# Attention and mixture of experts on one core: blocks gathered in quarters of rows and turned on VectorE, the norm's weight moved into the first layer's weights

## The chip, the cores and the metric

The kernel runs on one core of one Trainium2 chip. The metric is the time of one execution on the device in microseconds (us), the median over several runs; less is better.

The engines are named as in the profile: PE is TensorE's matmul (PEld its weight load), DVE is VectorE, ACT is ScalarE, POOL is GpSimd, SP is SyncE, which here only issues transfers. L711 is line 711 of the kernel before.

## The reference

Two stages. The first is linear attention without softmax over 8 batches, 8 heads, 576 positions and 64 dimensions, then a root-mean-square norm over the 64 dimensions with a weight `g_norm`:

```
kv  = einsum('bhsd,bhse->bhde', k, v)
out = einsum('bhsd,bhde->bhse', q, kv)
rms = sqrt(mean(out * out, axis=-1, keepdims=True) + 1e-6)
x   = out / rms * g_norm          # heads side by side: 4608 tokens x 512
```

The second is a mixture of experts: a token goes to one of 8 experts (a local gate may let it keep its predecessor's expert), and its output is

```
h      = maximum(x[b, s] @ w1[e], 0)      # 512 -> 1024
out    = p[e] * (h @ w2[e])               # 1024 -> 512
```

All data is float32. The kernel splits every operand of the expert layers in a high and a low part of type fp32r and adds three products (high·high, low·high, high·low).

## The kernel before

**Attention (about 0 to 130 us).** Groups of two batches: `kv` on PE (L346), turns of q (L406), the output (L427), and its sums of squares. The row of a token, not yet divided by its root mean square and without `g_norm`, is kept in `raw`, together with the reciprocals `r` of its 8 heads' root mean squares and 8 gates. 36 stores of 128 rows put them into the DRAM tile `xs`, 566 floats a row: 4 pieces of 128 values (two heads each) at a pitch of `PW` = 146, the reciprocals and gates in the space behind the first piece.

**Transfers on SP.** `fetch` (L169) issues everything that is not indexed on SP, in program order, and makes each wait for the seventh one before it (`LANES` = 7). Beside that the completion of transfers from SP and ACT is counted on eight semaphores in turn, and a transfer waits until the one before it on its semaphore has landed.

**Experts.** Expert 0 is done first, in four blocks, while routing ends. The other seven follow by load, as ranks 1 to 7 with the fixed widths 768, 704, 640, 608, 608, 576 and 512 tokens, that is 6, 6, 5, 5, 5, 5 and 4 blocks of up to 128 tokens. A rank takes its blocks in two parts, `la` and `lb` (3+3, 3+3, 2+3, 2+3, 2+3, 2+3 and 2+2): `first_wide` multiplies all tokens of `la` with w1, `second` multiplies each block with w2 (24 matmuls of 512 columns, 8 values of f by 3 products), then the same for `lb`. `ma` and `mb_` are the parts of the next rank.

A block passes these steps:

- `gather`: one indirect DMA on POOL (L711) brings 128 rows of 566 floats into a tile `xr` (6 buffers).
- `scale`: DVE multiplies the 512 values by the reciprocals (L724) and picks the gate `pe` (L1185, L1187).
- `turn`: four PE transposes of 128x128 into the PSUM tile `pt` (L734); ACT writes the high part, `pt` times `gcol` (L738, `gcol` is `g_norm` per partition); DVE writes the low part (L739). The results are `xh`, `xl` for one part of a rank and `yh`, `yl` for the other.
- at the end of `second`, ACT multiplies by the gate into `ot` (2 buffers, L909), and POOL scatters its rows to the output (L910).

The turns of the next part stand as hooks between the matmuls of `second`, so PE does a turn between two f.

**Weights.** Each rank needs 8 tiles of 128x1024 (4 of w1, 4 of w2). `wload` brings one into a staging tile `wst` (4 buffers), `wsplit` writes the high part on ACT (L221) and the low part on DVE (L225); the next load is issued when a staging tile comes free. A tile of w1 holds 128 consecutive input dimensions, one a partition.

**The order.** From expert 0's last block on the program stands in `manual_schedule`: PE, ACT, DVE and POOL execute in the order in which the code is written. The hooks and the places of the gathers in the loop over r set it. Before that, in the routing, the table `PASS` says at which point which helper runs.

Of the kernel before, what the change touches and what calls it, by code (L numbers as in the profile page):

```python
# [22 lines left out]
def kernel(  # L23
# [13 lines left out]
    P = 128  # L37
# [28 lines left out]
    XW = NP * PW - 2 * NG  # L66
# [7 lines left out]
    xs = dram.tile([NT, XW], F32, name="xs")  # L74
# [25 lines left out]
    gidr = const.tile([P, NR * KBM], I32, name="gidr")  # L100
    sidr = const.tile([P, NR * KBM], I32, name="sidr")
# [88 lines left out]
    def wfetch(t, e, i):  # L190

        if not isinstance(e, int):
            e = bass.ds(e, 1)
            if i < NW1:
# [6 lines left out]
        if i < NW1:  # L201
            fetch(t, w1[e, i * P:(i + 1) * P, :])
        else:
            f0 = (i - NW1) * 2 * P
            fetch(t.rearrange("p (a d) -> p a d", a=2),
                  w2[e, f0:f0 + 2 * P, :].rearrange("(a p) d -> p a d", p=P))

# [3 lines left out]
    def wsplit(e, i, two=False):  # L211
# [9 lines left out]
        nc.scalar.copy(hi, t)  # L221
        wt[e, i] = (hi, lo)

        def low(engine=nc.vector):
            engine.tensor_sub(lo, t, hi.bitcast(F32))  # L225
# [247 lines left out]
    def rows_out(g, raw, ms, kk):  # L473
# [49 lines left out]
        nc.vector.tensor_copy(raw[:, 0:n, XO + P:XO + P + H], r)  # L523
        nc.vector.tensor_mul(raw[:, 0:n, XO + P + H:XO + P + H + E], pe,
# [4 lines left out]
    def store(n=C):  # L529

        for _ in range(n):
            if not to_store:
# [4 lines left out]
                  raw[:, c, XO:XO + XW])  # L537
# [54 lines left out]
    def by_rank(ids, gi, si):  # L592
# [8 lines left out]
        make_idx(gi, si, tr, sm)  # L601

    def route(g, kk):
# [60 lines left out]
        def perms(n0, n1):  # L664
# [3 lines left out]
            if last:  # L668
# [7 lines left out]
                else:  # L676
                    assert "ranks" in done
                    by_rank(tid[:, ns], gidr, sidr)
# [9 lines left out]
        if last:  # L688
            ids(*cuts[1])
            yield  # L690
            perms(*cuts[1])
        elif g == 0:
# [16 lines left out]
    def gather(xr, idx, rows=NT, pin=False):  # L709
        assert len(stored) * P >= rows  # L710
        i = nc.gpsimd.indirect_dma_start(  # L711
            out=xr[:, 0:XW], out_offset=None, in_=xs[0:rows],
# [5 lines left out]

    def scale(xr, engine=None):

        xv = xr.rearrange("p (a w) -> p a w", a=NP)[:, :, 0:P].rearrange(
            "p a (x d) -> p a x d", x=2)
        r = xr[:, P:P + H].rearrange("p (a x) -> p a x", x=2)
# [3 lines left out]
    def gate(xr, e):  # L727
        return xr[:, P + H + e:P + H + e + 1]

    def turn(xr, xh, xl, t0, psum, tag="pt", pin=False, late=False):  # L730

        pt = psum.tile([P, ND, P], F32, name="pt", tag=tag)
        for d in range(ND):
            i = nc.tensor.transpose(pt[:, d], xr[:, d * PW:d * PW + P], ident)  # L734
# [156 lines left out]
    def products(pool, w, hh, hl, t0, pe, idx, psum, hooks=(), pin=False, m=P, late=False):  # L891
# [15 lines left out]
        def finish():  # L907
            ot = pool.tile([P, DM], F32, name="ot", bufs=2)
            nc.scalar.activation(ot[0:m], po[0:m], AF.Copy, scale=pe[0:m])  # L909
            nc.gpsimd.indirect_dma_start(  # L910
# [5 lines left out]
    def second(*a, **kw):  # L916
        products(*a, **kw)()
# [19 lines left out]
    def block(pool, w, t, pe, idx, psh, pst, psy, hooks, hs=None):  # L937
# [31 lines left out]
        second(pool, w, hh, hl, 0, pe, idx, psy, fs)  # L969
# [49 lines left out]
    PASS = dict(at.split(":") for at in "a0:2s22 a4:3 a6:223o33 b2:o b3:t c1:3 c2:x c3:3 c5:33T d1:3 d3:3 d4:f3 d5:r d8:3 d11:y d13:l d14:F".split())  # L1019

    def at(k):

        def do():
            for what in PASS[k]:
# [64 lines left out]
    def stream_block(op, e, t, idx):  # L1089
# [3 lines left out]
        def piece(i):  # L1093
# [3 lines left out]
            nc.scalar.copy(hi, st)  # L1097
            nc.vector.tensor_sub(lo, st, hi.bitcast(F32))
# [74 lines left out]
    class Block:  # L1173


        def __init__(self, r, kb, m=P):
            self.r, self.c, self.m = r, (r - 1) * KBM + kb, m

        def gather(self):
            self.xr = gather(xtile(xp, XB), cidx(gidr, self.c))  # L1180

        def scale(self):
            scale(self.xr)
            t = xp.tile([P, NR], F32, name="gs", bufs=2)
            nc.vector.tensor_mul(t, self.xr[:, P + H + 1:P + H + E], oneh[:, self.r - 1])  # L1185
# [3 lines left out]
        def turn(self, xh, xl, t0):  # L1189
            turn(self.xr, xh, xl, t0, ps_t)  # L1190
# [4 lines left out]
    def parts(r):  # L1195
# [3 lines left out]
        bl = [Block(r, k, min(P, n - k * P)) for k in range(-(-n // P))]  # L1199
# [12 lines left out]
    block(z, w, fourth, gate(fourth[0], 0), cidx(sidx, 3), ps_h, ps_t, ps_y,  # L1212
# [98 lines left out]
```

## Time and profile before

| measure | before |
|---|---|
| median of 3 runs | 599.58 us (597.09 to 602.48) |
| the profiled execution | 600.44 us, of which the span of its profile 598.7 us |
| PE busy | 558.3 us (93%) |
| DVE busy | 273.7 us (46%) |
| ACT busy | 237.9 us (40%) |
| POOL busy | 133.3 us (22%) |
| moved by DMA | 94.26 MB, mean 157 GB/s |

Busy times count instructions that are executing; issuing of transfers is in none of the five, but POOL's indirect DMAs, whose descriptors POOL writes itself, are in POOL's. A row of a timeline gives the start, the duration, the engine, the line, the operation with its tiles and, in brackets, how long the engine was idle before it and what ended that. On PE the durations of matmuls that follow one another overlap, so what one costs there is the distance between starts.

### The profile page before, as it was taken

The numbers are of one execution on the slowest core, as the hardware profiler recorded it, in microseconds if no ns is written. First come the engines' busy times: TensorE is split into PE (matmuls) and PEld (weight loads), VectorE is DVE, ScalarE is ACT, GpSimd is POOL, SyncE is SP. The second block draws the span as 40 slices with busy tenths as digits, with TensorE's granted clock in tenths as the row PEclk, the third lists the DMA queues.
The fourth block names the chain that finished last, engine by engine and source line by source line (L and its number), as shares of the span: only waits on it lengthen the run. The fifth ranks groups of instructions, "written<-read, shape, count | busy, mean of one in ns | idle before, by whom it ended". The sixth has DMA issues, their size and how long they took to land. (4 is left out here: it accounts for less than half of the span.)

```text
span 598.7 us, 12747 instructions
## 1 busy us (share of the span) xinstructions
PE 558.3 (93%) x5285; PEld 496.0 (83%) x5285; DVE 273.7 (46%) x539; ACT 237.9 (40%) x433; POOL 133.3 (22%) x200
## 2 busy tenths in 40 slices
PE   3888877869999999999999999999999999999996
PEld 3777766759887989898988898989798989988895
DVE  1128477769876436244342534444443625352410
ACT  1677766552254234233432333333333433442220
POOL 3333343233343021120302020202122011201001
PEclk9988889879999999999999999999999999999999
DMA  8999999570676334330623263515352444331000
GB/s 275 326 322 342 303 374 373 198 249 21 223 270 253 108 126 126 106 121 18 197 96 109 71 181 89 146 52 177 109 154 76 124 141 119 113 104 42 18 19 29
DMA packets 39906, 94.26 MB, mean 157 GB/s; under 512 B 5791, under 2 KB 5791, under 8 KB 39840
## 3 DMA queue, kind: packets, MB, share of 16 engines
q1 hardware_dynamic: 32320, 72.31, 36.3%
q0 software_dynamic: 6304, 21.04, 11.2%
q8 instruction: 43, 0.70, 0.5%
q10 hardware_dynamic: 1216, 0.02, 0.1%
q14 instruction: 23, 0.19, 0.1%
HBM read 73.48 MB, written 20.53 MB: 157 GB/s over the span
## 5 line engine op out<-in xcount | busy, mean ns | idle before, releaser
L921 DVE SCALAR_TENSOR_TENSOR hl<-ph,hh 128x384 fp32r<-128x384 f32 (+3 forms) x92 | 53.3, 580 | 144.1 <-ACT hh L920 118.1
L910 POOL DMA_INDIRECT out_dram<-ot,sidr x36 | 35.4, 984 | 336.5 <-ACT ot L909 336.5
L920 ACT ACTIVATE hh<-ph 128x384 fp32r<-128x384 f32 (+3 forms) x92 | 46.9, 510 | 130.2 <-PE ph L882 126.3
L909 ACT ACTIVATE ot<-py,pe 128x512 f32<-128x512 f32 (+2 forms) x39 | 26.8, 687 | 112.2 <-issue 54.9
L711 POOL DMA_INDIRECT xr<-xs,gidr x36 | 38.7, 1075 | 11.5 <-issue 9.9
L346 PE MATMUL po<-vt,kt 64*64 64x64 f32 x1152 | 25.9, 239 | 14.8 <-DMA vt<-in_v_dram 9.2
L471 DVE TENSOR_REDUCE ms<-sq 128x9 f32<-128x576 f32 x32 | 23.1, 750 | 32.4 <-POOL sq L466 26.6
L346 PEld LDWEIGHTS po<-vt,kt 64*64 64x64 f32 x1152 | 23.5, 153 | 14.1 <-issue 13.0
L427 PE MATMUL po<-kvb,qT 64*64 64x73 f32 x1024 | 28.2, 241 | 6.4 <-issue 5.6
L466 POOL TENSOR_TENSOR sq<-raw 128x576 f32<-128x576 f32 x16 | 20.5, 1285 | 60.5 <-ACT raw L436 21.0
L427 PEld LDWEIGHTS po<-kvb,qT 64*64 64x64 f32 x1024 | 22.7, 143 | 13.5 <-issue 9.2
L739 DVE SCALAR_TENSOR_TENSOR yl<-pt,gcol,yh 128x512 fp32r<-128x512 f32 x20 | 15.0, 751 | 36.7 <-ACT yh L738 36.7
L433 ACT COPY raw<-po 128x876 f32<-128x876 f32 (+1 forms) x32 | 20.8, 649 | 17.9 <-PE po L427 17.3
L367 POOL COPY kvb<-kvp 64x128 f32<-64x128 f32 x64 | 22.0, 343 | 17.4 <-ACT kvp L350 9.6
L724 DVE TENSOR_TENSOR xr<-xr 128x512 f32<-128x512 f32 x37 | 25.3, 683 | 0.6 <-DMA xr<-xs,gidr 0.6
L734 PEld LDWEIGHTS pt<-ident,xr 128*128 128x128 f32 x152 | 18.6, 140 | 6.6 <-issue 1.7
L734 PE MATMUL pt<-ident,xr 128*128 128x128 f32 x152 | 22.9, 273 | 1.0 <-issue 0.9
L406 PE MATMUL pq<-ident,qt 128*128 128x128 f32 x128 | 21.7, 318 | 2.0 <-ACT ql L387 1.0
L876 PE MATMUL py<-w_0h,hh 128*128 128x512 f32 (+2 forms) x58 | 23.5, 404 | 0.0
L876 PE MATMUL py<-w_1h,hh 128*128 128x512 f32 (+2 forms) x58 | 23.2, 399 | 0.0
L738 ACT ACTIVATE yh<-pt,gcol 128x512 fp32r<-128x512 f32 x20 | 13.8, 689 | 23.4 <-PE pt L734 23.4
L882 PE MATMUL py<-w_0h,hl 128*128 128x512 f32 (+2 forms) x58 | 22.9, 394 | 0.0
(359 smaller groups left out, 1661.4 us busy)
## 6 DMA issues: line engine op xcount, KB each, us to landing
wst<-in_moe_w_dram SPq DMA_DIRECT2D x64, 512.0 KB, 3.6
xs<-raw SPq DMA_DIRECT2D x36, 283.0 KB, 3.7
kt<-in_k_dram SPq DMA_DIRECT2D x32, 288.0 KB, 4.7
vt<-in_v_dram SPq DMA_DIRECT2D x32, 288.0 KB, 5.2
qt<-in_q_dram SPq DMA_DIRECT2D x32, 288.0 KB, 5.4
xr<-xs,gidr POOLq DMA_INDIRECT x36
out_dram<-ot,sidr POOLq DMA_INDIRECT x36
out_dram<-ot,si POOLq DMA_INDIRECT x3
```

Source lines behind the costliest of these rows:

```text
L346: nc.tensor.matmul(pk[half(x ^ b), x, 0:D], ks[b][half(x), cd], vs[b][half(x), cd], start=(c == 0), stop=(c == C - 1))
L427: nc.tensor.matmul(po[half(b), r, o:o + HW], lhsT[half(r), half(x)], kvb[half(r), slot(x, b):slot(x, b) + HW], start=True, stop=True)
L471: nc.vector.tensor_reduce(mss[g][:, :, 2 * n + x], sqs.pop((s, x)), axis=AX.X, op=ALU.add)
L711: i = nc.gpsimd.indirect_dma_start(out=xr[:, 0:XW], out_offset=None, in_=xs[0:rows], in_offset=bass.IndirectOffsetOnAxis(ap=idx, axis=0), ...
L724: (engine or nc.vector).tensor_mul(xv, xv, r.unsqueeze(3).to_broadcast([P, NP, 2, D]))
L734: i = nc.tensor.transpose(pt[:, d], xr[:, d * PW:d * PW + P], ident)
L876: mm = nc.tensor.matmul(ps, ah, bh, start=(first and i == 0), stop=False)
L882: nc.tensor.matmul(ps, al, bh, start=False, stop=(last and i == n - 1))
L909: nc.scalar.activation(ot[0:m], po[0:m], AF.Copy, scale=pe[0:m])
L910: nc.gpsimd.indirect_dma_start(out=outf, out_offset=bass.IndirectOffsetOnAxis(ap=idx[0:m], axis=0), in_=ot[0:m], in_offset=None, bounds_ch ...
L920: nc.scalar.activation(hh, ps, AF.Relu)
L921: nc.vector.scalar_tensor_tensor(hl, ps, 0.0, hh.bitcast(F32), op0=ALU.max, op1=ALU.subtract)
```

## The change

- **Rows of xs** get all 584 floats (4 x 146) in place of 566. The reciprocals of heads 2n and 2n+1 stand behind piece n, so a quarter of a row has its values and its two reciprocals; the 8 gates (`XE`) stand at a place of their own.
- **Gather by quarters.** A block of ranks 2 to 7 (30 blocks) is no longer brought by one indirect DMA of 128 rows x 566, but by `gather4`: four of 128 x 146, the u-th with the index table `gid4[:, u]`, and one of 128 x 8 for the gates. `gid4` is arranged so that partition 32q+k holds quarter q of the tokens 32u+k. Rank 1 (6 blocks) and expert 0 are gathered whole.
- **Turn on VectorE.** `turn4` takes the place of the four PE transposes in these 30 blocks: one DVE STREAM_TRANSPOSE in squares of 32x32 from `xr` into `xT` (one buffer), an ACT copy into the high part, a DVE subtraction into the low part. All are in SBUF. Input dimensions then lie on partitions in another order, (quarter, k mod 32) in place of 128 consecutive ones.
- **w1 in the same order.** For experts of ranks 2 to 7 a load of a w1 tile takes the rows in that order: the source's outermost dimension has 4 entries (steps of 131072, 1024 and 1 elements by 4, 32 and 1024) in place of one of 128.
- **g in the weights.** `split_w`: the high part of a w1 tile is `wst` times `g` (ACT ACTIVATE with a scale), the low part a SCALAR_TENSOR_TENSOR in place of the subtraction. The turns lose their `gcol`: ACT a plain copy, DVE a plain subtraction.
- **Index tables.** `sel_in` (4 DVE copies), `by_quarter` (4 PE matmuls of 128x36 and 2 DVE operations), one more DVE operation on `gidr`; 8 POOL memsets for `quart` and 4 small transfers for `gq` on ACT's queue at the start.
- **Places.** Gathers of the next rank's `la` stand at the rank's start (two) and behind `la`'s first `second` (the third); those of its `lb` before `first_wide(yt)` (two) and behind `lb`'s first `second`. In expert 0's last block the hook 13 turns block 0 first and scales block 2 after.

```
+    xs = dram.tile([NT, NP * PW], F32, name="xs")              # was XW = 566
+    for n in range(NP):
+        nc.scalar.dma_start(gq[n * QD:(n + 1) * QD], g_norm.rearrange("(x i) -> i x", i=QD))
...
+            if i < NW1 and quarters:
+                fetch(t, w1[e].rearrange("o (q j i) f -> j (o q) i f", j=NP, i=QD)[i])
...
+        g_ = gq[:, i % 2:i % 2 + 1] if quarters else gcol
+        nc.scalar.activation(hi, t, AF.Copy, scale=g_)
+        return lambda engine: engine.scalar_tensor_tensor(lo, t, g_, hi.bitcast(F32),
+                                                          op0=ALU.mult, op1=ALU.subtract)
...
+    def gather4(xr, c):
+        for idx, w, o in (*((gid4[:, u, c - KBM:c - KBM + 1], PW, u * PW) for u in range(NP)),
+                          (gidr[:, c:c + 1], E, NP * PW)):
+            src = xs.rearrange("t (q w) -> (t q) w", w=w)
+            i = nc.gpsimd.indirect_dma_start(
+                out=xr[:, o:o + w], out_offset=None, in_=src,
+                in_offset=bass.IndirectOffsetOnAxis(ap=idx, axis=0),
+                bounds_check=src.shape[0] - 1, oob_is_err=False)
...
+    def turn4(pool, xr, xh, xl, t0):
+        xT = pool.tile([P, ND, P], F32, name="xT", bufs=1)
+        nc.vector.transpose(
+            xT.rearrange("p j (u k) -> p u j k", k=QD),
+            pieces(xr).rearrange("p u (j i) -> p u j i", i=QD))
+        hi = xh[:, :, t0:t0 + P]
+        nc.scalar.copy(hi, xT)
+        nc.vector.tensor_sub(xl[:, :, t0:t0 + P], xT, hi.bitcast(F32))
...
-        nc.scalar.activation(hi, pt, AF.Copy, scale=gcol)
-        i = nc.vector.scalar_tensor_tensor(xl[:, :, t0:t0 + P], pt, gcol, hi.bitcast(F32),
-                                           op0=ALU.mult, op1=ALU.subtract)
+        nc.scalar.copy(hi, pt)
+        i = nc.vector.tensor_sub(xl[:, :, t0:t0 + P], pt, hi.bitcast(F32))
...
-           ... 13: [la[2].scale, turns[0]], 14: [turns[1]], 15: [turns[2]]}, hs=hs)
+           ... 13: [turns[0], la[2].scale], 14: [turns[1]], 15: [turns[2]]}, hs=hs)
...
-            for bl in ma:
+            for bl in ma[:2]:
                 bl.gather()
...
                 bl.second(w, hh, hl, x * P, hooks)
+                if not x and ma[2:]:
+                    ma[2].gather()
...
+            for bl in mb_[:2]:
+                bl.gather()
             first_wide(w, hh, hl, *yt, n=nb, then=then)
-            for bl in mb_:
-                bl.gather()
...
                 end = bl.second(w, hh, hl, x * P, hooks, not ma and left_ == 1)
+                if not x and mb_[2:]:
+                    mb_[2].gather()
```

On PE, in the part of a rank where `lb`'s blocks are multiplied with w2 and `ma` is turned (py is the output, w_0h and w_0l the parts of a w2 tile, hh and hl those of the hidden layer), one hook with a turn stood between two f of the same block, before:

```order
L876 MATMUL py<-w_0h,hh 128x512
L881 MATMUL py<-w_0l,hh 128x512
L882 MATMUL py<-w_0h,hl 128x512
L734 MATMUL pt<-ident,xr 128x128 x4
L876 MATMUL py<-w_0h,hh 128x512
L881 MATMUL py<-w_0l,hh 128x512
L882 MATMUL py<-w_0h,hl 128x512
L876 MATMUL py<-w_1h,hh 128x512
```

The same place of the changed kernel:

```order
L959 MATMUL py<-w_0h,hh 128x512
L964 MATMUL py<-w_0l,hh 128x512
L965 MATMUL py<-w_0h,hl 128x512
L959 MATMUL py<-w_0h,hh 128x512
L964 MATMUL py<-w_0l,hh 128x512
L965 MATMUL py<-w_0h,hl 128x512
L959 MATMUL py<-w_1h,hh 128x512
L964 MATMUL py<-w_1l,hh 128x512
```

The four transposes into pt are gone, and nothing stands in their place on PE.

On DVE, from the last scale of a part of a rank of rank 2 over its three turns to the next weight tile (xr is the gathered block, yl and yh the parts of the turned one), before:

```order
L724 TENSOR_TENSOR xr<-xr 128x4x128
L1185 TENSOR_TENSOR gs<-xr,oneh 128x7
L1187 TENSOR_REDUCE pe<-gs 128x1
L739 SCALAR_TENSOR_TENSOR yl<-pt,gcol,yh 128x4x128 x3
L225 TENSOR_TENSOR w_4l<-wst,w_4h 128x1024
```

And the same place of the changed kernel:

```order
L807 TENSOR_TENSOR xr<-xr 128x4x128
L1274 TENSOR_TENSOR gs<-xr,oneh 128x7
L1276 TENSOR_REDUCE pe<-gs 128x1
L796 STREAM_TRANSPOSE xT<-xr 128x4x4x32
L801 TENSOR_TENSOR yl<-xT,yh 128x4x128
L796 STREAM_TRANSPOSE xT<-xr 128x4x4x32
L801 TENSOR_TENSOR yl<-xT,yh 128x4x128
L796 STREAM_TRANSPOSE xT<-xr 128x4x4x32
L801 TENSOR_TENSOR yl<-xT,yh 128x4x128
L232 SCALAR_TENSOR_TENSOR w_4l<-wst,gq,w_4h 128x1024
```

A transposition has come ahead of each subtraction, and the next one on DVE stands behind the subtraction of the block before it.

On POOL, from one part's scatters (out_dram) over the gathers to the next, for a rank with parts of two and three blocks, before:

```order
L910 DMA out_dram<-ot,sidr 4608x512 x3
L711 DMA xr<-xs,gidr 128x566 x2
L910 DMA out_dram<-ot,sidr 4608x512 x2
L711 DMA xr<-xs,gidr 128x566 x3
L910 DMA out_dram<-ot,sidr 4608x512 x3
```

And in the changed kernel (gid_88 is `gid4`):

```order
L993 DMA out_dram<-ot,sidr 4608x512 x3
L780 DMA xr<-xs,gid_88 128x146 x4
L780 DMA xr<-xs,gidr 128x8
L780 DMA xr<-xs,gid_88 128x146 x4
L780 DMA xr<-xs,gidr 128x8
L993 DMA out_dram<-ot,sidr 4608x512
L780 DMA xr<-xs,gid_88 128x146 x4
L780 DMA xr<-xs,gidr 128x8
L993 DMA out_dram<-ot,sidr 4608x512 x2
```

Where two or three gathers stood between scatters there are now ten, and five more between the first and the second scatter of a part.

On SP, in the first loads (kt, vt, qt are tiles of k, v and q; a DMAHW name is one of the eight semaphores on which transfers of SP and ACT are counted in turn), from the fifth load on, before:

```order
L169 DMA qt<-in_q_dram 128x576 [waits DMAHW0_49]
L169 DMA qt<-in_q_dram 128x576 [waits DMAHW1_49]
L169 DMA kt<-in_k_dram 128x576 [waits DMAHW2_49]
L169 DMA vt<-in_v_dram 128x576 [waits DMAHW3_49]
L169 DMA kt<-in_k_dram 128x576 [waits DMAHW4_49]
L169 DMA vt<-in_v_dram 128x576 [waits DMAHW5_49]
```

And in the changed kernel:

```order
L184 DMA qt<-in_q_dram 128x576 [waits DMAHW0_49]
L184 DMA qt<-in_q_dram 128x576 [waits DMAHW2_49]
L184 DMA kt<-in_k_dram 128x576 [waits DMAHW4_49]
L184 DMA vt<-in_v_dram 128x576 [waits DMAHW6_49,DMAHW1_49]
L184 DMA kt<-in_k_dram 128x576 [waits DMAHW0_49]
L184 DMA vt<-in_v_dram 128x576 [waits DMAHW1_49]
```

The four transfers of gq take semaphores in between, so the second kt of this piece now waits for the first qt (DMAHW0), and the last vt stands behind it.

## Rows read from the trace of the kernel before

**Rows 1.** Busy time of each engine by stretch, with clock and DMA share.
```profile
core 0: us, PE busy (x) PEld busy (x) DVE busy (x) ACT busy (x) POOL busy (x), PEclk, DMA share, GB/s
80.00:100.00 20.00, 16.52 (x480) 14.44 (x473) 14.12 (x37) 13.67 (x35) 8.79 (x17) 0.92 1.04 379
...
255.00:321.00 66.00, 66.00 (x358) 58.57 (x358) 25.92 (x44) 22.42 (x36) 12.08 (x11) 1.00 0.34 109
...
379.00:436.00 57.00, 57.00 (x336) 51.11 (x336) 24.48 (x40) 20.74 (x31) 10.09 (x10) 1.00 0.41 124
```

**Rows 2.** All waits of PE from 186 to 590: us, times, longest.
```profile
PE ph L881 <- issue: 0.3, 1, 0.3
```

**Rows 3.** Timeline of PE around one turn in the second layer.
```profile
334.09 0.39 PE L882 MATMUL py<-w_1h,hl 128*128 128x512 f32 x1
334.32 0.60 PE L734 MATMUL pt<-ident,xr 128*128 128x128 f32 x4
334.68 0.48 PE L876 MATMUL py<-w_1h,hh 128*128 128x512 f32 x1
...
335.23 0.40 PE L882 MATMUL py<-w_1h,hl 128*128 128x512 f32 x1
```

**Rows 4.** Groups by line and form: busy us, mean ns, idle before.
```profile
L724 DVE TENSOR_TENSOR xr<-xr 128x512 f32<-128x512 f32 x37 | 25.3, 683 | 0.6 <-DMA xr<-xs,gidr 0.6
L739 DVE SCALAR_TENSOR_TENSOR yl<-pt,gcol,yh 128x512 fp32r<-128x512 f32 x20 | 15.0, 751 | 36.7 <-ACT yh L738 36.7
L738 ACT ACTIVATE yh<-pt,gcol 128x512 fp32r<-128x512 f32 x20 | 13.8, 689 | 23.4 <-PE pt L734 23.4
L225 DVE TENSOR_TENSOR w_0l<-wst,w_0h 128x1024 fp32r<-128x1024 f32 x10 | 12.3, 1233 | 4.7 <-ACT w_0h L221 4.7
L221 ACT CAST w_0h<-wst 128x1024 fp32r<-128x1024 f32 x10 | 10.4, 1040 | 0.0
```

**Rows 5.** Timeline of POOL: a scatter, three gathers, the next scatter.
```profile
345.83 0.99 POOL L910 DMA_INDIRECT out_dram<-ot,sidr  x1 [5.40 <-ACT ot L909]
347.13 1.05 POOL L711 DMA_INDIRECT xr<-xs,gidr  x1 [0.30 <-PE ph L882]
348.48 1.02 POOL L711 DMA_INDIRECT xr<-xs,gidr  x1 [0.31 <-issue]
...
368.92 1.01 POOL L910 DMA_INDIRECT out_dram<-ot,sidr  x1 [18.12 <-ACT ot L909]
```

**Rows 6.** Timelines of POOL and of DVE at 258: the longest gather.
```profile
258.50 2.04 POOL L711 DMA_INDIRECT xr<-xs,gidr  x1 [0.31 <-issue]
...
258.42 1.23 DVE L225 TENSOR_TENSOR w_4l<-wst,w_4h 128x1024 fp32r<-128x1024 f32 x1 [0.38 <-issue]
```

**Rows 7.** Weight loads: landing times, their queue's share, two casts four loads apart.
```profile
DMA to landing us min/median/max: 3.5/3.6/6.8
...
q1 hardware_dynamic: 32320, 72.31, 36.3%
...
324.29 1.04 ACT L221 CAST w_2h<-wst 128x1024 fp32r<-128x1024 f32 x1
...
349.38 1.04 ACT L221 CAST w_1h<-wst 128x1024 fp32r<-128x1024 f32 x1
```

**Rows 8.** Timelines of SP's issues and of PE at the start.
```profile
4.51 0.80 SPq L169 DMA_DIRECT2D qt<-in_q_dram  x2
...
8.86 0.33 SPq L169 DMA_DIRECT2D vt<-in_v_dram  x1
...
13.39 0.92 PE L346 MATMUL po<-vt,kt 64*64 64x64 f32 x24 [0.92 <-DMA vt<-in_v_dram]
```

**Rows 9.** Timelines of PE and DVE where rank 1 begins.
```profile
183.40 0.66 PE L734 MATMUL pt<-ident,xr 128*128 128x128 f32 x4 [0.87 <-issue]
...
185.62 0.44 PE L881 MATMUL ph<-xl,w_4h 128*128 128x384 f32 x1 [0.35 <-issue]
...
184.81 0.75 DVE L739 SCALAR_TENSOR_TENSOR xl<-pt,gcol,xh 128x512 fp32r<-128x512 f32 x1 [0.81 <-issue]
```

More of the change, by code (lines that the diff above doesn't have):

```diff
@@ L100 @@
     gidr = const.tile([P, NR * KBM], I32, name="gidr")
+    gid4 = const.tile([P, NP, NR * KBM - KBM], I32, name="gid4")
+    quart = const.tile([P, 2], F32, name="quart")
+    for n in range(NP):
+        nc.gpsimd.memset(quart[n * QD:(n + 1) * QD, 0:1], float(n))
+        nc.gpsimd.memset(quart[n * QD:(n + 1) * QD, 1:2], float(n - NP))
     sidr = const.tile([P, NR * KBM], I32, name="sidr")
@@ L601, in by_rank, with sel_in, by_quarter @@
         make_idx(gi, si, tr, sm)
+        gi = gi[:, KBM:]
+        nc.vector.tensor_scalar(gi, gi, NP * PW // E, XE // E, op0=ALU.mult, op1=ALU.add)
+        return tr
+    trs = []
+    def sel_in():
+        sel.append(z.tile([P, DM], F32, name="sel", tag="ot", bufs=2).rearrange(
+            "p (u m) -> p u m", u=NP))
+        for u in range(NP):
+            nc.vector.tensor_copy(sel[0][:, u].rearrange("p (q k) -> p q k", k=QD),
+                                  ident[:, u * QD:(u + 1) * QD].unsqueeze(1).to_broadcast([P, NP, QD]))
+    sel = []
+    def by_quarter():
+        n = NR * KBM - KBM
+        pq4 = rbank[:, 128:128 + NP * n].rearrange("p (u n) -> p u n", n=n)
+        for u in range(NP):
+            nc.tensor.matmul(pq4[:, u], sel[0][:, u], trs[0][:, KBM:], start=True, stop=True)
+        t = sm.tile([P, NP, n], F32, name="q4", tag="co")
+        nc.vector.tensor_scalar(t, pq4, float(NP), quart[:, 1:2], op0=ALU.mult, op1=ALU.add)
+        nc.vector.tensor_scalar(gid4, t, quart[:, 0:1], None, op0=ALU.max)
     def route(g, kk):
@@ L691, in route @@
             perms(*cuts[1])
+            yield
+            by_quarter()
         elif g == 0:
@@ L711, in gather @@
         i = nc.gpsimd.indirect_dma_start(
-            out=xr[:, 0:XW], out_offset=None, in_=xs[0:rows],
+            out=xr, out_offset=None, in_=xs[0:rows],
             in_offset=bass.IndirectOffsetOnAxis(ap=idx, axis=0),
@@ L1044, in do @@
                     read_ranks()
+                elif what == "z":
+                    sel_in()
                 elif what == "l":
@@ L1173, with __init__ @@
     class Block:
-        def __init__(self, r, kb, m=P):
-            self.r, self.c, self.m = r, (r - 1) * KBM + kb, m
+        def __init__(self, r, kb, m=P, whole=False):
+            self.r, self.c, self.m, self.whole = r, (r - 1) * KBM + kb, m, whole
         def gather(self):
-            self.xr = gather(xtile(xp, XB), cidx(gidr, self.c))
+            self.xr = xp.tile([P, NP * PW + E], F32, name="xr", bufs=XB)
+            if self.whole:
+                gather(self.xr[:, 0:NP * PW], cidx(gidr, self.c))
+            else:
+                gather4(self.xr, self.c)
         def scale(self):
@@ L1189, in turn @@
         def turn(self, xh, xl, t0):
-            turn(self.xr, xh, xl, t0, ps_t)
+            if self.whole:
+                turn(self.xr, xh, xl, t0, ps_t)
+            else:
+                turn4(xp, self.xr, xh, xl, t0)
         def second(self, w, hh, hl, t0, hooks=(), last=False):
@@ L1198, in parts @@
         na = HM if n > 2 * HM - P else 2 * P
[L1199 removed]
+        bl = [Block(r, k, min(P, n - k * P), r == 1) for k in range(-(-n // P))]
         return bl[:na // P], bl[na // P:], na, n - na
@@ L1211 @@
     turns = [lambda x=x, bl=bl: bl.turn(*xt, x * P) for x, bl in enumerate(la)]
-    block(z, w, fourth, gate(fourth[0], 0), cidx(sidx, 3), ps_h, ps_t, ps_y,
+    i = block(z, w, fourth, gate(fourth[0], 0), cidx(sidx, 3), ps_h, ps_t, ps_y,
           {2: [split[0]], 4: [split[1]], 7: [split[2]], 8: [split[3]],
-           **{11 + x: [bl.scale] for x, bl in enumerate(la[:2])}, 13: [la[2].scale, turns[0]], 14: [turns[1]], 15: [turns[2]]}, hs=hs)
+           **{11 + x: [bl.scale] for x, bl in enumerate(la[:2])}, 13: [turns[0], la[2].scale], 14: [turns[1]], 15: [turns[2]]}, hs=hs)
+    behind.append(i)
     hand.close()
```

60 lines of the change are left out of this document (37 added, 23 removed).

## The prediction

> **What bounds the kernel now.** I read the windows first. The attention stage is limited by transfers: from 80 to 100 us the DMA engines are busy all the time (share 1.04) at 379 GB/s while PE, DVE and ACT have idle time [rows 1]. In the expert stage it is PE: from 255 to 321 and from 379 to 436 its busy time is the whole window, at granted clock 1.00, while DVE has 24.5 of 57 us, ACT 20.7 and POOL 10.1, and the DMA share is 0.41 [rows 1]. The list of PE's waits confirms it: in 404 us from 186 on one wait of 0.3 us [rows 2]. So whatever is taken from PE there is taken from the end, as long as nobody else becomes late; what is added to DVE, ACT and POOL costs nothing while it fits beside PE's work.
>
> **Turns taken from PE.** Matmuls of 512 columns start 0.23 us apart (334.09 to 334.32). From 334.09 to 335.23 there are three of them and one turn, 1.14 us, so the turn costs 1.14 − 3 x 0.23 = 0.45 us [rows 3]. Its transposes alone take 0.36 (334.32 to 334.68); the rest is the matmul behind it, which starts late. 30 blocks lose their turn: 30 x 0.45 = −13.5 us. The lower bound is 30 x 0.36 = 10.8, if the slow start belongs to the change of f and stays. A rank of five blocks so goes from 57 us to 57 − 5 x 0.45 = 54.7.
>
> **What DVE and ACT get for it.** A subtraction over 128x512 takes 0.68 us as a two-operand form (L724) and 0.75 with a pointer (L739), so the low part is hardly cheaper; ACT's 0.69 stays [rows 4]. In a w1 tile DVE's form with a pointer replaces the plain one; by the same two rows that is +0.07 per 512 columns, 0.15 a tile of 1.23; ACT's cast of 1.04 per 1024 columns becomes an ACTIVATE with a scale, which takes 0.69 per 512 (from PSUM), so at most 1.4 [rows 4]. The transposition on DVE is in no row. Nearest are passes of DVE over the same 128x512 values, 0.68 to 0.75 [rows 4]; from below one pass, from above one such pass for each of the four quarters, 2.7 us. I take 1.2, nearer the single pass, since it is one instruction. DVE then has per rank 24.5 + 5 x 1.2 + 4 x 0.15 = 31 of 54.7 us: hidden on the average. The Trainium skill (VectorE: DVE Perf Modes, The three transpose paths) gives 311 ns for 128x128 in bf16, an estimate of 1.24 us for four; no run here shows it yet.
>
> It is tight in one place. `xT` has one buffer, so the turns of `lb` in ranks 3 to 6 make a chain: after the first block of `la` ends, ACT does `ot` (0.69), the copy of block 1 (0.69), DVE its subtraction (0.68), the transposition d, ACT's copy (0.69), DVE's subtraction (0.75), together 3.5 + d, and `first_wide` wants the result one block of 24 x 0.23 = 5.5 us later [rows 3, 4]. With some hand-overs it holds up to d = 1.8. At 1.2 it costs 0, at 2.7 it costs 4 ranks x 0.9 = 3.6 us.
>
> **Gathers on POOL.** A gather of 128 rows takes 1.05 and 1.02 us, a scatter of rows of another size 0.99, and starts lie 1.35 apart: the price is per instruction, not per byte [rows 5]. A quarter should cost the same. Per rank of five blocks that is 25 gathers and 5 scatters, 30 x 1.33 = 40 us of 54.7. Starts can be held up: one gather took 2.04 where DVE's weight split, with two operands from SBUF, ran from 258.42 to 259.65 [rows 6]. DVE has such operations (8 weight tiles, 5 scales, 5 low parts, 5 transpositions) for 8 x 1.23 + 10 x 0.68 + 5 x 1.2 = 22.6 of 54.7 us; a start falls into one with chance 0.41 and waits half of some 1 us, 30 x 0.41 x 0.5 = 6 us more. 46 of 54.7 still fits. Between the scatters there is room: POOL was idle for 18.12 us before the scatter at 368.92 [rows 5], and ten gathers take 13.3. The five that now stand between the first and the second scatter of a part (6.7 us against a block of 5.5) delay that scatter by about 2 us; `ot` has two buffers, so ACT waits for nothing. Cost 0; its bound is the rival below.
>
> **Loads of w1.** Their source's outermost dimension has four entries. A staging tile is written again every four casts: 324.29 to 349.38, 25 us for a load that now lands in 3.6 (3.5 to 6.8) [rows 7]. Cost 0 while landing plus queueing fits; its bound is the rival below.
>
> **Start.** The last vt of the first set is issued at 8.86 and PE waits for such a tile until 13.39, so a landing takes about 4.5 us [rows 8]. In the changed kernel the kt ahead of it waits for the qt of 4.51 [rows 8], which lands at about 9.0 to 9.9, and vt goes out behind it; its own semaphore may belong to a gq transfer that lands later still. Attention is limited by transfers, so a later start moves all of it: +1.5 us, between 0 (the queues make it up) and 3.
>
> **Smaller terms.** The stores of `xs` grow by 18 floats a row, 36 x 128 x 72 bytes = 0.33 MB; half of them fall in the stretch limited by transfers, 0.17 MB at 379 GB/s [rows 1]: +0.5 us (0 to 1). `by_quarter` adds four matmuls of 36 columns, about a turn: +0.5. Where rank 1 begins PE waits 0.87 us for the third block's scale and 0.35 for its low part, since DVE stood at a scale that waited [rows 9]; the swap at hook 13 and a low part without `gcol` take back some 0.9, longer weight splits just before give 0.3: −0.6. The 8 memsets on POOL and the copies of `sel_in` lie beside transfers and other work.
>
> **The sum.** −13.5 + 1.5 + 0.5 + 0.5 − 0.6 = −11.6. The profiled execution took 600.44 us (its span 598.7), 0.86 above the median of 599.58. 600.44 − 11.6 = 588.8, and put on the median's level 588.0.
>
> **The rivals.**
> - *The saving is mostly eaten.* A turn is worth 0.36, the start costs 3, the transposition takes the chain to 4 x 0.9 = 3.6 us of stalls: −10.8 + 3 + 3.6 + 0.4 = −3.8, about 596. For it: DVE and ACT hand over twice per block. Against: three terms at their ends at once. 0.11.
> - *POOL sets the pace; slower.* With every start held up as in the longest row, 2.04 + 0.31 = 2.35 us [rows 6], 30 DMAs take 70.5 us a rank, 15.8 over 54.7. Five ranks with gathers of the next one: 588 + 5 x 15.8 = 667. It decides from 54.7 / 30 = 1.82 us per DMA on. Against: the undisturbed starts are 1.30 and 1.35 apart [rows 5], and the held one lies beside one particular DVE operation. 0.07.
> - *w1 arrives late; slower.* If a load ran on four of the 16 DMA engines only, it would move 128 KB on each. The queue moved 72.31 MB in 36.3% of 16 x 598.7 = 3477 us, 20.8 GB/s per engine [rows 7]: 6.3 us. A load now has 32 KB on each, 1.6 us of its 3.6, so 2.0 lie around it: 8.3 in all. From above, four times 3.6 is 14.4. PE is late if the four tiles of w1 and four of w2, with three or four in flight, don't pass in 54.7 us: (54.7 − 4 x 3.6) / 4 = 10.1 us per load, were they one after the other. At 14.4 it is 72 us per rank, +17 x 6 ranks = 104, about 692; at 8.3 nothing. 0.07. The Trainium skill (DMA: Bandwidth & Descriptors, Why a DMA increments its semaphore by 16 and not by 1) says that the slowest dimension sets the number of engines, the largest count up to 16 that divides it, which would be four here; no row shows such a transfer, and the sum by it is still 588, unless the load is slower than 10.1 us.
>
> **How the numbers follow.** The forecast has 0.75: 588.0, its own range 584.5 (start and stores at 0, DVE's chain free, 0.5 a turn) to 592.5 (0.36 a turn, start at 3). The eaten saving has 0.11, the slower rivals 0.07 each. The range of 8 in 10 is 583 to 596, which leaves out the slower rivals and the ends of the rest. A change of 1%, 6 us, is about what a measurement of this kernel can tell from none (593.6 and 605.6): faster 0.76 (the forecast and a little of the eaten saving), same 0.11, slower 0.13 (the rest of both).
>
> **What would show it.** Right: windows of five-block ranks of about 54.7 us with PE busy all through, no row of PE waiting for `yl`, `xl` or weights, POOL at about 40 us a rank with gathers 1.3 to 1.5 apart, casts of w1 tiles that don't wait for a DMA, PE's first matmul at 14 to 16 us. Wrong: PE waiting for ACT's or DVE's part of a turned block (the chain; then the transposition is above 1.8 us); scales waiting for gathers (POOL); ACT casts waiting for `wst` (w1 loads); or a rank of 57 us with no wait at all (a turn cost nothing).

## The result

| | before | changed |
|---|---|---|
| median of all runs | 598.12 us (594.73 to 603.03, 20 runs) | 597.87 us (586.91 to 609.13, 20 runs) |
| the profiled execution | 600.44 us, span 598.7 | 593.96 us, span 591.9 |
| POOL busy | 133.3 us (22%) | 273.9 us (46%) |

The ratio is 0.9875, interval 0.984 to 0.9911: faster by 1.25%, which on the median of before in the prediction is 592 us. The comparison counts only runs within 1.5% of the fastest of a kernel, which for the kernel before are all and for the changed one 8 of 20, because its times spread over 22 us. The medians of all 20 are level, 598.12 and 597.87. So there are two results: what the change saves where nothing disturbs it (predicted: 588.0), and something that takes a changing part of it back, here all of it in the median. The experiments show the first at 585.7 us and the second as a thing that was there on some chips and not on others.

The windows of the changed kernel in the expert stage, with the columns of [rows 1]:

```profile
255.00:321.00 66.00, 61.98 (x317) 53.85 (x317) 28.40 (x48) 20.27 (x32) 34.15 (x32) 0.97 0.37 110
321.00:379.00 58.00, 55.20 (x308) 49.20 (x307) 28.01 (x45) 20.47 (x30) 28.80 (x28) 1.00 0.34 104
379.00:436.00 57.00, 56.68 (x324) 50.27 (x323) 27.83 (x45) 20.41 (x31) 35.84 (x34) 1.00 0.45 131
```

The second of these windows in the kernel before, which [rows 1] do not show:

```profile
321.00:379.00 58.00, 58.00 (x336) 52.81 (x335) 24.72 (x40) 20.83 (x31) 10.05 (x10) 1.00 0.40 115
```

PE is no longer busy all through: 4.0, 2.8 and 0.3 us are missing, where the kernel before has none. DVE went up by 2.5 to 3.4 us, POOL from 10 to 12 us per window to between 29 and 36. All waits of PE from 186 to 590, against the one of 0.3 us in [rows 2]:

```profile
PE py L959 <- ACT hh L1003: 4.0, 1, 4.0
PE py L959 <- issue: 2.1, 2, 1.9
PE ph L959 <- ACT yh L800: 0.4, 1, 0.4
PE ph L959 <- DVE hl L1004: 0.3, 1, 0.3
PE ph L964 <- DVE yl L801: 0.3, 1, 0.3
```

The longest stands in the second layer, for `hh`, the hidden layer's high part, which ACT writes with its relu from `ph`. Timelines of PE (the last matmuls of the seventh and eighth f of `first_wide`, then the wait), ACT and POOL around it:

```profile
265.58 0.33 PE L965 MATMUL ph<-xh,w_3l 128*128 128x384 f32 x1
267.66 0.33 PE L965 MATMUL ph<-xh,w_3l 128*128 128x384 f32 x1
...
272.44 0.40 PE L965 MATMUL py<-w_5h,hl 128*128 128x512 f32 x1
276.86 0.79 PE L959 MATMUL py<-w_5h,hh 128*128 128x512 f32 x1 [4.02 <-ACT hh L1003]
277.45 0.63 PE L964 MATMUL py<-w_5l,hh 128*128 128x512 f32 x1
277.88 0.63 PE L965 MATMUL py<-w_5h,hl 128*128 128x512 f32 x1
...
263.87 0.49 ACT L1003 ACTIVATE hh<-ph 128x384 fp32r<-128x384 f32 x1 [1.59 <-PE ph L965]
269.18 0.49 ACT L1003 ACTIVATE hh<-ph 128x384 fp32r<-128x384 f32 x1 [4.81 <-PE ph L965]
276.32 0.49 ACT L1003 ACTIVATE hh<-ph 128x384 fp32r<-128x384 f32 x1 [6.65 <-remote]
...
260.42 0.99 POOL L993 DMA_INDIRECT out_dram<-ot,sidr  x1 [5.00 <-ACT hh L1003]
261.71 1.04 POOL L780 DMA_INDIRECT xr<-xs,gid  x1 [0.30 <-issue]
...
273.49 0.99 POOL L780 DMA_INDIRECT xr<-xs,gidr  x1 [0.30 <-issue]
```

The matmuls of the eighth f ended at 268.0; the relu that waits for nothing but them began at 276.32, with ACT idle since 269.67. In the trace's semaphore events PE's signals for the seventh and eighth f stand at 269.15 and 276.30, 3.2 and 8.3 us after the matmuls' ends; in the kernel before such a signal stands 0.01 to 0.02 us after its matmul. While it lasted POOL issued a scatter and ten gathers, 1.3 us apart, from 260.42 to 274.5. Behind the wait PE has another loss: its matmuls start 0.43 us apart instead of 0.23 for some 3 us, at a granted clock of 0.51 (the lower of its two levels, 1.2 GHz) where it had 1.00 before the 4 us in which it stood still. In the windows of these stretches:

```profile
264.00:272.00 8.00, 8.00 (x43) 7.22 (x42) 2.79 (x8) 0.86 (x2) 6.06 (x7) 1.00 0.39 123
272.00:276.80 4.80, 0.84 (x4) 0.37 (x2) 0.00 (x0) 0.48 (x1) 1.99 (x2) 0.97 0.17 32
276.80:280.00 3.20, 3.14 (x8) 2.48 (x8) 2.44 (x6) 1.08 (x3) 0.00 (x0) 0.51 0.00 0
```

### The profile page after: what moved, and what is told of

It reads as the page before. It is cut to its first block, busy times and chain, and to the rows that moved or that the text cites. A ratio compares the mean times of both kernels' runs of the same rounds, so it can differ in the third digit from the quotient of the medians.

```text
span 591.9 us, 12820 instructions
## 1 busy us (share of the span) xinstructions
PE 549.0 (93%) x5173; PEld 483.4 (82%) x5173; DVE 298.1 (50%) x576; ACT 236.0 (40%) x433; POOL 273.9 (46%) x328
## 4 chain that ended last, share of the span: by engine, by line
PE 70%; DMA 9%; issue 9%; DVE 4%; POOL 3%; ACT 2%; another core or an unknown queue 1%; SPq 0%; POOLq 0%; DVEq 0%
PE ph L965 10%; PE ph L964 10%; PE ph L959 10%; PE py L959 10%; PE py L965 9%; PE py L964 9%; PE po L454 3%; DMA wst<-in_moe_w_dram 3%; POOL xr L780 3%; PE po L373 3%; DMA out_dram<-ot,sidr 2%; PE pq L433 2%; DMA xr<-xs,gidr 1%; PE pm L420 1%
## 5 line engine op out<-in xcount | busy, mean ns | idle before, releaser
L780 POOL DMA_INDIRECT xr<-xs,gid x120 | 133.4, 1112 | 36.6 <-issue 33.5
L993 POOL DMA_INDIRECT out_dram<-ot,sidr x36 | 38.2, 1060 | 154.5 <-ACT ot L992 97.9
L373 PE MATMUL po<-vt,kt 64*64 64x64 f32 x1152 | 27.8, 252 | 13.0 <-DMA vt<-in_v_dram 9.9
L780 POOL DMA_INDIRECT xr<-xs,gidr x30 | 33.2, 1107 | 9.1 <-issue 8.8
L373 PEld LDWEIGHTS po<-vt,kt 64*64 64x64 f32 x1152 | 25.7, 165 | 14.2 <-issue 11.4
L394 POOL COPY kvb<-kvp 64x128 f32<-64x128 f32 x64 | 24.0, 374 | 16.6 <-ACT kvp L377 9.7
L959 PE MATMUL py<-w_5h,hh 128*128 128x512 f32 (+2 forms) x52 | 21.0, 404 | 4.2 <-ACT hh L1003 4.0
L964 PE MATMUL py<-w_1l,hh 128*128 128x512 f32 (+2 forms) x58 | 22.6, 390 | 0.1
L964 PE MATMUL py<-w_0l,hh 128*128 128x512 f32 (+2 forms) x58 | 22.7, 391 | 0.0
L965 PE MATMUL py<-w_1h,hl 128*128 128x512 f32 (+2 forms) x58 | 22.7, 391 | 0.0
```

Of the source, the lines that this page charges most:

```text
L373: nc.tensor.matmul(pk[half(x ^ b), x, 0:D], ks[b][half(x), cd], vs[b][half(x), cd], start=(c == 0), stop=(c == C - 1))
L394: copy[KVB[t]](pair(kvbs[s][half(t)], slot(0, y) + XO, slot(1, 1 - y), D), kvps[s][half(y)])
L780: i = nc.gpsimd.indirect_dma_start(out=xr[:, o:o + w], out_offset=None, in_=src, in_offset=bass.IndirectOffsetOnAxis(ap=idx, axis=0), boun ...
L959: mm = nc.tensor.matmul(ps, ah, bh, start=(first and i == 0), stop=False)
L964: nc.tensor.matmul(ps, ah, bl, start=False, stop=False)
L965: nc.tensor.matmul(ps, al, bh, start=False, stop=(last and i == n - 1))
```

## The experiments

Three theories at the start: POOL's gathers hold up PE's signals, by their number or by the length of a run (theory POOL); the w1 loads with four entries outermost do it; the chain on DVE and ACT does it. Later a fourth: chips differ. A relu is called late where it begins over 0.4 us after its matmuls have ended and ACT has nothing else to do; its lateness is that idle time. The twelve runs fell on four chips, called A to D here; kernels of one chip shared the runs of the kernel before, whose median was 598.8, 598.7, 598.6 and 600.0 us on A to D.

### Chip A: the changed kernel again

No edit.

> The changed kernel once more, beside the experiments on the same chip. In its first profile PE waited 7 us in the expert stage (before: 0.3), above all at 272.8 and 336.4, where ACT's relu came 3 to 6 us after the matmuls that it needs, each time while POOL was writing gathers. If this comes from POOL's gathers or from the DMA engines, it falls at other places in every execution: the times spread over some 20 us again (586 to 608), and this profile shows late relus at other times, 2 to 8 us each, all beside gathers. If it is a fixed stall of the order of instructions, the same two places show it and the times agree within 0.3%.

Measured: 594.1 us (586.0 to 611.1, 6 runs), ratio 0.9842 (0.9765 to 0.9919). Late relus at 229, 233, 235, 269, 326, 349, 354, 355, 398, 466 and 469, 0.7 to 3.8 us each, inside or just behind runs of 11 or 12 POOL transfers; PE's longest wait, 3.6 us, was for `yh` this time. Some places come again (the first profile has late relus at 230, 236, 269 and 276 too), but the longest waits stand elsewhere, and the times spread as before. So it is no fixed stall of the order.

### Chip A: whole gathers

```
             else:
-                gather4(self.xr, self.c)
+                i = gather(self.xr[:, 0:NP * PW], cidx(gidr, self.c), ins=True)
...
```

> Each block of ranks 2 to 7 is gathered by one indirect DMA of 128x584 in place of four of 128x146 and one of 128x8; the turn on DVE, the w1 order and g stay. (The rows then reach the turn in another order than the w1 tiles.) POOL theory: the late relus come from runs of five to ten gathers; with 30 instead of 150 they go, PE has no waits after 190, and the time is the changed kernel's 594 less 7 us of waits and some 2 us at the lower clock: 585, agreeing within 4 us. If w1's loads on few DMA engines or the DVE turn are the cause: no change, 587 to 608, late relus as before.

Measured: 584.7 us (583.4 to 588.5, 7 runs), ratio 0.9753 (0.9714 to 0.9791). From 190 on PE has no wait in the list; its window, with POOL at 11.6 us:

```profile
321.00:379.00 58.00, 58.00 (x338) 53.29 (x337) 28.48 (x46) 21.26 (x33) 11.60 (x10) 1.00 0.38 119
```

As theory POOL expected, within 0.5 us. The w1 loads with four entries and DVE's turn are still in this kernel, so alone they are not the cause.

### Chip A: without the gates' gather

```
-        for idx, w, o in (*((gid4[...], PW, u * PW) for u in range(NP)),
-                          (gidr[:, c:c + 1], E, NP * PW)):
+        for idx, w, o in tuple((gid4[...], PW, u * PW) for u in range(NP)):
```

> The DMA of 128x8 for the gates is left out (another column is read as the gate), the four of 128x146 stay: 120 gathers instead of 150. If the small rows of 32 bytes hold up PE's signals (the late ones were released when a gate's gather landed): no late relus, 585 us and a small spread. If the length of a run of gathers on POOL does it: four fifths of the runs' length, late relus stay, somewhat fewer, 587 to 604. If w1's loads do it: no change.

Measured: 588.1 us (581.9 to 596.7, 6 runs), ratio 0.9824 (0.9778 to 0.987). Late relus stay, eight in the profile, up to 2.5 us, in or just behind runs of nine transfers. So the rows of 32 bytes are not needed for them. PE waited only 0.7 us after 186 in this profile, and it took 581.9 us: a late relu costs something only where PE runs out of other work. That there is less of it with 120 gathers than with 150 is not shown, since the times overlap with those of the changed kernel beside it (586.0 to 611.1).

### Chip A: the kernel before with more gathers

```
             self.xr = gather(xtile(xp, XB), cidx(gidr, self.c))
+            if self.r > 1:
+                xq = xp.tile([P, NP * PW], F32, name="xq", bufs=1)
+                for u in range(NP):
+                    nc.gpsimd.indirect_dma_start(out=xq[:, u * PW:(u + 1) * PW], ...)
```

> The kernel before, with four gathers of 128x146 into an unused tile added to each of the 30 blocks of ranks 2 to 7, nothing else. POOL theory: the changed kernel's stalls come from the gathers alone, so they appear here too: late relus beside runs of five to fifteen gathers, PE waits of some us, times 600 to 615 with a spread of over 10 us. If w1's loads on four engines, the DVE turn or the 32-byte rows are the cause: the time of before, 598, within 0.5%, and no late relus.

Measured: 608.7 us (603.4 to 622.0, 6 runs), ratio 1.0154 (1.0094 to 1.0214). ACT's timeline shows late relus, here with 2.52 us of idle time ahead of one for which the matmuls had ended 1.2 us before, beside a run of seven POOL transfers:

```profile
295.58 0.44 ACT L920 ACTIVATE hh<-ph 128x320 fp32r<-128x320 f32 x1 [0.39 <-PE ph L882]
298.55 0.44 ACT L920 ACTIVATE hh<-ph 128x320 fp32r<-128x320 f32 x1 [2.52 <-PE ph L882]
...
291.32 0.97 POOL L910 DMA_INDIRECT out_dram<-ot,sidr  x1 [4.56 <-ACT ot L909]
...
297.87 1.00 POOL L1184 DMA_INDIRECT xq<-xs,gidr  x1 [0.30 <-issue]
299.18 1.00 POOL L711 DMA_INDIRECT xr<-xs,gidr  x1 [0.30 <-issue]
```

So the gathers alone, in a kernel that has nothing else of the change, cost 10 us in the median and bring the spread. How much of the 10 us is late signals and how much later scales was not separated.

### Chip B: w1 in the old order of rows

```
-        wfetch(t, by[e], i, e > 1)
+        wfetch(t, by[e], i)
```

> The changed kernel with w1 loaded as before (128 consecutive rows, source dimension of 128 outermost); all else as changed, so the 150 gathers and the DVE turn stay (the weights then stand in another order than the turned rows). POOL theory: nothing changes, times 586 to 608, late relus beside runs of gathers. If the w1 loads in four pieces hold up anything (late weights, PE's signals): the stalls shrink and the time falls towards 585.

Measured: 584.5 us (583.0 to 588.8, 4 runs), ratio 0.978 (0.9723 to 0.9836), no wait of PE from 186 on, no late relu, though POOL's runs are of 11 and 12 as in the changed kernel. Against theory POOL, it seemed; I took it that w1's loads and gathers must come together. That fell on chips C and D.

### Chip B: pauses, and POOL busy with something else

A pause after each block's gathers, or two per block (`PAUSES` is `(0,)` or `(0, 3)`):

```
+            if len(done4) % NP5 in PAUSES and done4:
+                tc.add_manual_dep(i.ins, done4[-1].ins.name, ...Sync...)
+            done4.append(i)
```

> The changed kernel; the first gather of each block on POOL waits until the last gather of the block before has landed (some 2.2 us after its start in place of 1.3), so POOL writes runs of at most five gathers, and of six with a scatter. In the four profiles with many gathers all late relus lie in or just behind runs of seven or more POOL transfers and begin some 5 us after a run's start; in runs of up to four there is none. If the length of a run decides: hardly any late relus, 585 to 589 us with a spread of some 5 us. If the number of gathers decides, at any pace: as the changed kernel, 586 to 608.

> As with the pause per block, but a second pause within each block, so runs of two and three gathers, 11 pauses of about 1 us a rank: POOL needs 25 x 1.3 + 10 x 1 + 5 x 1.3 = 49 of 54.7 us a rank. If the length of a run decides: no late relus at all; 585 to 588 us, unless scales now wait for gathers (then DVE's row for the scale shows a DMA wait and PE waits for it, some us a rank). If the number of gathers decides: 586 to 608.

Whole gathers with memsets ahead:

```
+                for _ in range(2 * NP):
+                    nc.gpsimd.memset(self.xr, 0.0)
                 i = gather(self.xr[:, 0:NP * PW], cidx(gidr, self.c), ins=True)
```

> The kernel with whole gathers (584.7 us) with eight POOL memsets of 128x592 ahead of each of the 30 gathers, about 0.6 us each, so POOL is busy in runs as long as with quarters, but writes no descriptors in them. If writing of descriptors or its transfers hold up PE's signals: as whole gathers, 584 to 588, no late relus. If any long POOL work does: late relus, 587 to 608.

Measured: 594.4 us (587.5 to 603.0, 6 runs) with one pause, 661.7 us (654.3 to 665.9, 6 runs) with two, 585.1 us (584.1 to 588.5, 4 runs) with memsets; no late relus in any. Since a kernel with unbroken runs of 11 has none on chip B either, the three say nothing on what makes signals late. What they show is the price of a pause. In the kernel with two, POOL's waits for landings and DVE's for gathered blocks are

```profile
POOL xr L780 <- DMA xr<-xs,gid: 81.9, 29, 6.4
...
POOL xr L780 <- DMA xr<-xs,gidr: 42.0, 13, 6.7
...
DVE xr L811 <- DMA xr<-xs,gid: 24.1, 8, 5.3
```

and PE waits behind them for `hl`, up to 11.4 us at once. I had reckoned 1 us a pause; these 42 are 2.95 us on average, up to 6.7, because a gather lands later than I thought (in this trace 3.0 us after its start in the median, where I had 2.2).

### Chip C: w1 by four transfers a tile

```
-                fetch(t, w1[e].rearrange("o (q j i) f -> j (o q) i f", j=NP, i=QD)[i])
+                for n in range(NP):
+                    r0 = n * P + i * QD
+                    fetch(t[n * QD:(n + 1) * QD], w1[e, r0:r0 + QD, :]..., n > 0)
```

> The changed kernel complete, only that each w1 tile of ranks 2 to 7 is loaded by four transfers of 32 rows, each with 32 entries outermost, in place of one with 4 outermost; the same bytes go to the same places. With the old order of rows (150 gathers, runs of 11 and 12) PE did not wait and nearly all 16 landing signals per gather were recorded (15.8), with the four-entry loads 6.0 and gathers landed 1.1 us later. If it is the four-entry loads together with the gathers that make PE's signals late: 584 to 585 us, spread of some 5 us, no late relus, gathers landing in about 3 us. If the old order of rows itself mattered (128 rows in a row of DRAM): 590 or more.

Measured: 596.1 us (587.3 to 602.1, 13 runs), ratio 0.9957 (0.9933 to 0.9981). Late relus all over, up to 4.0 us late and up to 4.5 us behind their matmuls; of 16 landing signals per gather 5.4 are recorded. A miss: loads with 32 entries outermost don't cure it, so four entries are no condition of it.

### Chip C: the kernel before with w1's loads alone changed

```
-                fetch(t, w1[e, i * P:(i + 1) * P, :].rearrange("o p f -> (o p) f"))
+                fetch(t, w1[e].rearrange("o (q j i) f -> j (o q) i f", j=4, i=32)[i])
```

> The kernel before, with its w1 loads of ranks 1 to 7 in the order of the change (four entries outermost), nothing else (the weights then stand in another order than the turned rows). If these loads were late for ACT's casts by themselves: over 605 us. If they do harm only together with long runs of gathers: 598 us, no late relus, but the whole gathers land later than before (median 3.8 us there), 5 to 7 us as in the kernel with whole gathers and such loads (7.3).

Measured: 622.0 us (618.4 to 622.7, 6 runs), ratio 1.0389 (1.036 to 1.0419). A miss again, but in one place: rank 1, which the change leaves out. Its casts on ACT wait for the loads:

```profile
174.52 1.05 ACT L221 CAST w_4h<-wst 128x1024 fp32r<-128x1024 f32 x1 [5.88 <-DMA wst<-in_moe_w_dram]
185.71 1.05 ACT L221 CAST w_5h<-wst 128x1024 fp32r<-128x1024 f32 x1 [9.65 <-DMA wst<-in_moe_w_dram]
192.20 1.05 ACT L221 CAST w_6h<-wst 128x1024 fp32r<-128x1024 f32 x1 [4.96 <-DMA wst<-in_moe_w_dram]
197.80 1.05 ACT L221 CAST w_7h<-wst 128x1024 fp32r<-128x1024 f32 x1 [4.06 <-DMA wst<-in_moe_w_dram]
```

The last two come 6.5 and 5.6 us after the one before: that is what such a load of 512 KB takes when they stand in a row. From rank 2 on no cast waits, the windows are full (57.00 of 57.00), and there is no late relu.

### Chip D: both on one chip

No edit, and the edit of the first kernel on chip B.

> The changed kernel again, beside the one with w1 in the old order of rows, on one chip. The latter took 584.5 us with no late relu and nearly all landing signals recorded, but on another chip than the changed kernel's runs, and the four transfers per tile, with 16 DMA engines each, still gave 587 to 602. Theory one: the order of rows of w1 matters in some way, then this kernel shows 587 to 608, late relus, some 6 of 16 landings recorded. Theory two: chips differ in how much a run of gathers holds up PE's signals; then both kernels show the same here, either 583 to 589 with 15 to 16 landings recorded or 587 to 608 with some 6.

> The changed kernel with w1 in the old order of rows, as before (the weights then stand in another order than the turned rows), now on the same chip as the changed kernel. If the order of w1's rows matters: 583 to 589 us and no late relu here, while the changed kernel beside it has 587 to 608. If the chip does: the same as the changed kernel beside it, within 2 us in the median.

Measured: the changed kernel 585.7 us (584.0 to 587.9, 6 runs), ratio 0.9772 (0.9743 to 0.9801); with the old order of rows 586.1 us (584.2 to 587.8, 6 runs), ratio 0.9779 (0.9749 to 0.9808). The changed kernel has no wait of PE from 186 on. Its windows, and ACT and POOL at the place where it stood still on the first chip:

```profile
379.00:434.00 55.00, 55.00 (x321) 49.19 (x320) 28.40 (x46) 20.59 (x31) 32.81 (x31) 1.00 0.44 129
```

```profile
267.40 0.49 ACT L1003 ACTIVATE hh<-ph 128x384 fp32r<-128x384 f32 x1 [1.59 <-PE ph L965]
269.48 0.49 ACT L1003 ACTIVATE hh<-ph 128x384 fp32r<-128x384 f32 x1 [1.59 <-PE ph L965]
...
266.86 1.00 POOL L780 DMA_INDIRECT xr<-xs,gid  x1 [0.30 <-issue]
268.17 1.00 POOL L780 DMA_INDIRECT xr<-xs,gid  x1 [0.30 <-issue]
...
272.33 1.00 POOL L780 DMA_INDIRECT xr<-xs,gidr  x1 [0.30 <-issue]
```

The same run of gathers, at the same pace, and the relus come 2.08 us apart as their matmuls do. Theory two, then: the chip decides, as far as these runs can tell. The same kernel takes 585.7 us with a spread of 3.8 on D and 594.1 with a spread of 25 on A. On A 30 gathers take 584.7 us, 120 take 588.1 and 150 take 594.1, of which 30 and 150 differ (one of the six times with 150 lies in the range of the seven with 30), while 120 is told apart from neither. On B it doesn't matter: 584.5 us with 150, 585.1 with 30 and memsets.

Whether it is the number of gathers or the length of a run, the traces of the first two profiles, A and C say in part. Of the 328 relus in or within 2 us behind a run of seven or more POOL transfers 59 are late, of the 133 at shorter runs and the 236 elsewhere none. Inside one trace, that of the kernel before with more gathers, it is 17 of 60 against none of 18 at runs of one to five. That speaks for the length; no run changed the length alone on such a chip.

**What stays open.** What distinguishes the chips, and by which way a gather on POOL reaches a signal of PE, no run tells. Each of A to D was used in one stretch of time only, so what is put down to the chip can be something else that differed between these stretches. One trait goes with it: of the 16 landing signals per gather the traces of the changed kernel hold 6.0 (first profile), 6.2 (A) and 15.9 (D), worked out from the semaphore events from 190 to 550; with whole gathers on A it is 16.0. POOL's scatters sort all fourteen traces: 11.3 to 13.2 of 16 in the eight of the first two profiles, A and C, 15.9 to 16.0 in the six of B and D. Three of the eight have no late relu (the kernel before, whole gathers, w1's loads alone), so the trait is not a result of late relus, and by it B is of D's kind. Signals lost from a trace raise a rival that no run tests: every timed execution was a traced one, so recording may have a part in the delay. Whether shorter runs help on a chip of A's kind is open too, since the kernels with pauses fell on chip B.

## Why the prediction was right, and where not

**Turns taken from PE: right, a little too small.** On D, from the first matmul of rank 1 to the last on PE, the expert stage takes 393.3 us where it took 408.3, in the profile of the whole gathers on A too: −15.0, 0.50 us for each of the 30 turns if all of it is put down to them (predicted 0.45). The five-block ranks, from the first matmul of one to that of the next, went from 57.9, 56.7, 56.8 and 55.3 to 55.2, 54.6, 53.9 and 52.9 (predicted 57 to 54.7).

**DVE and ACT: right, the transposition priced too high.** The list of the tile `xT` on D, and the groups by line:

```profile
L796 DVE STREAM_TRANSPOSE xT<-xr x30: 699/704/712, 238.1 to 549.5; 128x512 f32<-128x512 f32 x30
```

```profile
L801 DVE TENSOR_TENSOR yl<-xT,yh 128x512 fp32r<-128x512 f32 x17 | 11.8, 692 | 14.0 <-ACT yh L800 14.0
...
L800 ACT CAST yh<-xT 128x512 fp32r<-128x512 f32 x17 | 10.5, 617 | 25.8 <-DVE xT L796 25.8
```

The transposition takes 0.70 us, one pass over the data, at the lower bound; I took 1.2. The estimate of 1.24, four times the 311 ns for 128x128 in bf16 of the Trainium skill (VectorE: DVE Perf Modes, The three transpose paths), doesn't agree with the trace either. The chain has room up to 1.8 us, and on D PE waited neither for `yh` nor for `yl`. A w1 tile's low part takes 1.28 to 1.29 us (predicted 1.23 + 0.15, [rows 4]).

**POOL: the pace was right, the conclusion not.** Gathers of 146 floats start 1.30 us apart, those of 566 did 1.35 [rows 5], and POOL is busy for 32.8 of 55 us. The rival priced it as a bound on pace, from 1.82 us per DMA on, and that never came. The step that failed is the sentence of the first part that what is added to POOL costs nothing while it fits beside PE's work. POOL's work fitted, and on some chips its long runs of gathers still delayed signals from PE to ACT, which none of the rivals had. On A that took back what lies between the 584.7 us with whole gathers and the 586 to 611 of the changed kernel.

**w1's loads: right, by cover.** They cost nothing in ranks 2 to 7: with and without, 585.7 and 586.1 us on one chip. In a row they take 5.6 to 6.5 us, near the 6.3 worked out from [rows 7]. The rule in the Trainium skill (DMA: Bandwidth & Descriptors, Why a DMA increments its semaphore by 16 and not by 1), by which the slowest dimension sets the number of engines, four here, agrees with that. The traces of D show a difference in the landing signals too: loads of w1 in the new order have 5, nearly all in the old order 16. What I left out is whom else they delay: a gather lands 5.0 us after its start with them and 3.0 without (medians from the semaphore events on D). The cover of some 25 us per load [rows 7] explains why it cost nothing, and rank 1 without that cover shows the price: its first matmul on PE came at 207.0 us instead of 184.8, and the time was 622.0.

**Start and smaller terms: not to be told.** The last vt was issued at 9.51 in the first profile (8.86 in [rows 8]; predicted behind a landing at 9.0 to 9.9), and PE began its second piece there at 14.16 instead of 13.39. But rank 1 begins at 184.8 us in the profile of before, at 179.2 in that of the same code with more gathers, and between 180.7 and 184.1 in three of the changed kernel: the attention stage varies by more than all these terms together.

**The sum.** Predicted 11.6 us less; on B and D, without the disturbance, it is 14.2 to 14.3 (598.7 − 584.5, where the order of w1's rows was the old one, and 600.0 − 585.7), so 2.6 to 2.7 more. The turns gave 1.5 of that. The rest, 1.1 to 1.2, comes from the smaller terms: I had put them at 1.9 in all (1.5 for the start, 0.5 for the stores, 0.5 for `by_quarter`, −0.6 where rank 1 begins), and 15.0 − 14.3 leaves 0.7 on D. No profile shows them one by one. The recorded ratio, worth 592 us, is this less a part that the disturbance took back. That it lies so near to 588.0 is partly luck: the forecast had no disturbance, and the median of all 20 executions there, 597.87, lies outside its range of 583 to 596. On D all six times lie inside.

## What to carry to other kernels

Work that moves off a saturated engine is worth its distance between starts on that engine (0.50 us here), if what takes it has cover; so look for the place that has no cover (rank 1's loads) before a transfer is made slower. A spread that grows from 8 to 22 us is a result in itself: find who was late in one profile, and run an experiment and its control on the same chip before a cause is named, since here a comparison across two chips first pointed to the wrong one. Prefer few large indirect transfers to many small ones even where POOL has room: their price per instruction is the same, and on some chips late signals came with long runs of them.

## What the runs showed of the hardware

- On some chips, during or just behind runs of seven and more indirect transfers on POOL, 1.3 us apart, signals from PE's matmuls reached ACT late, by 0.4 to 8.3 us (59 of 328 relus); at shorter runs none was seen (of 133). On other chips, B and D, runs of 11 and 12 did nothing. All of it is from traced executions.
- After a standstill of PE of 4.0 us the granted clock was 0.51 for some 3 us, and matmuls of 512 columns started 0.43 us apart.
- A transposition in squares of 32 over 128x512 float32 values takes DVE 0.70 us, like a subtraction of that size (0.69).
- An indirect DMA costs POOL the same 1.0 us (median from 190 us on) for 128 rows of 32, 584 and 2264 bytes; single ones took up to 2.0.
